# An attention and gated-MLP kernel: more products of ones ahead of the steps, the last tile in three pieces, and a new order of all steps

## The chip, the cores and the metric

The kernel runs on one core of a Trainium2 chip. The metric is device time of one execution in microseconds (us). A core has a matrix engine (TensorE, PE in the profile, with its weight loads shown apart as PEld), a vector engine (VectorE, DVE), a scalar engine that evaluates functions (ScalarE, ACT), a general engine (GpSimd, POOL) and a queue that here issues all transfers (SyncE, SP). Each works through its own queue in order, and they wait for each other by semaphores.

## The reference

Eight batches, each with eight heads of 576 positions and 64 channels. Attention is linear: the softmax of q runs over a row's 64 channels, that of k over the 576 positions, and the 64 by 64 matrix of k and v is formed before q meets it. The result of all heads, 576 by 512, goes through a gated MLP whose gate mixes positions.

```python
q_s = softmax(q, over channels); k_s = softmax(k, over positions)
kv  = einsum('bhsd,bhse->bhde', k_s, v)
x   = einsum('bhsd,bhde->bhse', q_s, kv)       # laid out as (8, 576, 512)
h   = gelu_tanh(x @ w_in)                      # 512 -> 1024
u, v = h[..., :512], h[..., 512:]
v_n = (v - mean(v)) / sqrt(var(v) + 1e-6) * g_ln
v_s = einsum('ts,bsd->btd', w_sg, v_n) + b_sg[None, :, None]
out = x + (u * v_s) @ w_out
```

## The kernel before, in words

Everything is written as small steps, one Python function each, and a table of text, PLAN, names the steps in the order in which they are issued, with their numbers (batch, head or tile) and sometimes a letter for the engine (V is DVE, A is ACT, G is POOL). Each engine's queue is in the order of that table: DVE, ACT, POOL and SP are chained by the class InOrder (line 154 of the profile's rows), and TensorE by `mm` (line 241). So the table decides what stands behind what, and waits between engines follow from which step reads or writes which tile.

The dense products run in a reduced form of float32 with each operand split into a high and a low part, so a product is three products (`x_h` by `wi_h`, `x_h` by `wi_l`, `x_l` by `wi_h`). For each batch the steps are: `load_q`, `load_k`, `load_v`; the softmax steps `q_max`, `q_sub`, `q_exp`, `q_sum`, `q_inv`, `q_mul`, `q_turn` and `k_sub`, `k_exp`; `kv_mm` with `kv_inv` and `kv_scale`; `x_mm` with `x_high` and `x_low`; `hv_mm` and `hv_gelu` for the half v, its normalisation, `hu_mm` and `hu_gelu` for the half u; `sg_mm` and `gate` for the mixing of positions; `out_mm`, `out_add`, `out_rest` and `out_store`. The steps of several batches are interleaved.

Batches 0 and 1 start differently, since nothing else can cover them. For batch 0, `k0_max`, `k0_less` and `k0_mm` take the maximum of k over positions, the exponential (on ACT) and a transposition on TensorE by products with the identity `eye`; `k0_copy` brings the result from PSUM to SBUF. `q0_turn` transposes q in the same way and `q0_copy` copies it. `x0_mm`, `x0_high`, `x0_neg`, `x0_low` form x and its two parts. The weights `w_in` come in eight pieces, which `wi_a` (ACT), `wi_b`, `wi_d` (DVE), `wi_h` and `wi_l` turn into a high and a low part; `wi_x` does one of them on TensorE. The u half of batch 0 is made by `hu0_mm f j s`: tile f of four, half j of the positions, half s of the channels. Four calls with one f fill one PSUM tile, and `hu0_gelu f j` (ACT) reads half j of that tile. All early exponentials on ACT (`k0_less`, `q_exp`) stand ahead of the first gelu, which needs another function table (ACT_TABLE_LOAD).

PSUM is held in three tiles of two banks (`ps2`, shown as ps_0_78, ps_1_79 and ps_2_80) and two of one bank (`ps1`, ps_0_81 and ps_1_82), taken in turn by `bank`. A wait stands between a reader of such a tile and its next writer, also where they touch different halves of it.

Ahead of all steps TensorE multiplies a tile of ones (`vn_1[0]`, set by POOL) with itself 18 times; nothing reads the result. At the end, tile 3 of the last batch's output is made in two halves of 288 columns by `last_mm`, `last_add` and `last_store`, both in one PSUM tile.

Of the kernel before, what the change touches and what calls it, by code (L numbers as in the profile page):

```python
# [38 lines left out]
load_w_in 2, k0_copy 0 2, k0_less 0 1, q0_mul 1 1, wi_a 3, wi_b 3, load_v 0 0, neg, q0_turn 1 1, q0_copy 1 1, load_w_in 0, kv_mm 0 1, k0_copy 0 0
q0_turn 0 0, kv_inv 0 1, q0_copy 0 0, kv_scale 0 1, q0_mul 1 0, wi_a 2, wi_d 1, load_q 1 0, wi_d 3, k0_mm 0 1, k0_copy 0 1, q0_turn 1 0, load_q 1 1  # L40
x0_mm 1 1, load_w_in 6, x0_high 1 1, kv_mm 0 0, wi_b 2, wi_d 2, kv_inv 0 0, x0_neg 1 1, q0_copy 1 0, load_w_in 7, x0_mm 1 0, kv_scale 0 0
x0_low 1 1 A, wi_h 3 V, x0_high 1 0, wi_h 1 V, wi_l 1, x0_mm 0 1, x0_mm 0 0, wi_h 2 V, x0_neg 1 0, wi_x 2, x0_high 0 1, x0_neg 0 1, load_w_in 5
x0_low 1 0 A, hu0_mm 1 0 1, hu0_mm 1 1 1, q_max 1 0, q_max 1 1, wi_a 0, wi_b 0, q_swapm 1 0, x0_low 0 1 A, hu0_mm 1 1 0, load_w_in 4, q_top 1 0
load_k0 1 1, wi_d 0, wi_h 0 V, x0_high 0 0, x0_neg 0 0, wi_x 0, wi_l 3, wi_a 6, q_sub 1 0 V, wi_l 2 A, hu0_mm 3 0 1, hu0_mm 3 1 1, x0_low 0 0 A
wi_l 0 A, q_swapm 1 1 G, wi_b 6, wi_a 4, q_top 1 1, q_exp 1 0, wi_d 6, wi_h 6, hu0_mm 1 0 0, q_sub 1 1 V, q_exp 1 1, load_k0 1 0, wi_b 4, hu0_mm 2 0 1
hu0_mm 2 0 0, hu0_mm 2 1 1, wi_d 4, load_k0 1 2, load_k0 1 3, k0_max 1 2, wi_h 4, k0_less 1 2, k0_max 1 3, k0_less 1 3, load_v 1 1, k0_max 1 1
k0_less 1 1, k0_max 1 0, hu0_mm 3 1 0, wi_l 6, hu0_mm 2 1 0, hu0_mm 3 0 0, wi_l 4 V, q_sum 1 0, q_swapd 1 0 G, k0_less 1 0, hu0_gelu 2 0, hu0_gelu 1 0
q_sum 1 1, q_swapd 1 1 G, q_inv 1 0, load_w_out 2, hu0_gelu 3 0, hu0_gelu 2 1, hu0_gelu 1 1, load_w_sg 2, hv_mm 0 2, hv_mm 0 3, load_w_out 0
k0_mm 1 0, q_mul 1 0 1 V, q_turn 1 1, hu0_gelu 3 1, k0_mm 1 1, hv_gelu 0 2 A, hv_gelu 0 3, k0_mm 1 3, q_inv 1 1, hv_mm 0 0, q_mul 1 1 0, load_g
k0_copy 1 1, load_w_out 1, k0_copy 1 0, wo_a 0, load_kt 2 1, q_mul 1 0 0 V, q_turn 1 0, hv_gelu 0 0 A, q_turn 1 2, load_v 1 0, k0_mm 1 2, load_w_out 3  # L50
k0_copy 1 2, wo_b 0, k0_copy 1 3, wo_d 0, wo_a 2, q_mul 1 1 1, kv_mm 1 0, kv_inv 1 0, kv_scale 1 0, kv_mm 1 1, q_turn 1 3, x_mm 1 0, load_q 2 0
hv_sq 0 0, wo_b 2, hu0_mm 0 0 1, load_v 2 0, kv_inv 1 1, kv_scale 1 1, x_high 1 1, wo_d 2, hv_sq 0 2, x_high 1 0, x_low 1 1, hu0_mm 0 1 1, load_w_sg 3
hv_stat 0 2 A, x_low 1 0, hv_mm 0 1, x_mm 1 1, hv_gelu 0 1, load_q 2 1, x_high 1 2, hv_stat 0 0 A, hu0_mm 0 1 0, load_w_sg 1, hv_stat 0 3, hv_norm 0 3
load_w_sg 0, hv_stat 0 1, hv_norm 0 2, load_kt 2 0, hv_pow 0 2, x_low 1 2, x_high 1 3, x_low 1 3, ws_h 0, hv_norm 0 0, hv_pow 0 3, ws_l 0 V
hv_high 0 2, load_b, hv_low 0 2, hv_high 0 3, hv_low 0 3, load_w_sg 4, hu0_mm 0 0 0, hu0_gelu 0 0, ws_h 2, load_k 2 0, hv_mm 0 4, hv_gelu 0 4 A
hv_norm 0 1, hv_pow 0 0, hv_high 0 0, hv_mm 1 1, hv_gelu 1 1 A, ws_l 2 V, hv_mm 1 2, hv_mm 1 3, hv_low 0 0, b_h, hv_gelu 1 2 A, ws_h 4 V, hv_sq 0 4
hv_pow 0 1, hv_high 0 1, load_k 2 1, kt_max 2 0, ws_l 4, hv_norm 0 4, hv_stat 0 4 A, hv_pow 0 4, tail_high 0, tail_again 0, hv_mm 1 0, kt_max 2 1
tail_low 0, hv_low 0 1, hu0_gelu 0 1, load_kt 2 3, b_l, tail_high 1, load_kt 2 2, q_max 2 1, hv_sq 1 1, q_swapm 2 1, wo_h 0, wo_l 0 V, hv_sq 1 2
hv_stat 1 2 A, hv_norm 1 1, hv_gelu 1 3, sg_mm 0 0, gate 0 0, tail_low 1, kt_max 2 2, sg_mm 0 1, sg_mm 0 2, wo_h 2, hv_gelu 1 0 A, gate_high 0 0
hv_sq 1 0, load_v 2 1, gate 0 2, hv_stat 1 3, gate 0 1, gate_high 0 1, q_top 2 1, sg_mm 0 3, gate_low 0 0, hv_norm 1 2, gate_high 0 2, gate_low 0 1  # L60
hu_mm 1 0, gate_low 0 2 G, kt_max 2 3, hv_pow 1 2, gate 0 3, gate_high 0 3, kt_put 2, hv_stat 1 1 A, hv_high 1 2, hv_stat 1 0 A, hv_pow 1 0
hv_pow 1 3, wo_l 2, hv_norm 1 0, gate_low 0 3, out_mm 0 0, hv_norm 1 3, hu_gelu 1 0, out_mm 0 1, q_max 2 0, q_swapm 2 0, q_top 2 0, out_mm 0 3
out_add 0 0, out_add 0 1, hv_pow 1 1, kt_get 2, hv_high 1 1, k_sub 2 1, out_add 0 3, hv_low 1 2, hv_high 1 0, out_mm 0 2, hu_mm 1 1, load_kt 3 0
hv_low 1 1, hu_mm 1 2, q_sub 2 1 V, q_sub 2 0, out_add 0 2, q_exp 2 0, q_sum 2 0, hv_low 1 0, q_swapd 2 0 G, k_exp 2 1, hu_gelu 1 1, k_sub 2 0
q_exp 2 1, out_rest 0 3, q_inv 2 0, q_mul 2 0 0 V, hv_high 1 3, q_sum 2 1, hu_gelu 1 2, q_mul 2 0 1, q_turn 2 1, k_exp 2 0, hv_low 1 3, q_swapd 2 1 G
kt_max 3 0, load_kt 3 1, kt_max 3 1, load_kt 3 3, kt_max 3 3, q_inv 2 1, out_rest 0 2, out_rest 0 1, load_kt 3 2, kt_max 3 2, tail_again 1, hu_mm 1 3
sg_mm 1 0, kv_mm 2 0, q_turn 2 0, load_k 3 0, q_mul 2 1 0 V, kv_inv 2 0, kv_scale 2 0, q_mul 2 1 1 V, q_turn 2 3, kv_mm 2 1, kt_put 3, hu_gelu 1 3
sg_mm 1 2, gate 1 2, gate 1 0, gate_high 1 2, sg_mm 1 1, gate 1 1, gate_high 1 0, q_turn 2 2, x_mm 2 0, sg_mm 1 3, x_high 2 0, out_rest 0 0
x_high 2 1, kv_inv 2 1, x_low 2 1, x_low 2 0, gate_low 1 0 G, gate_high 1 1, gate_low 1 1 G, gate_low 1 2 G, kv_scale 2 1, gate 1 3, kt_get 3
k_sub 3 0, gate_high 1 3, load_q 3 0, x_mm 2 1, x_high 2 3, gate_low 1 3, load_v 3 0, x_high 2 2, x_low 2 2, out_mm 1 0, x_low 2 3, hv_mm 2 0  # L70
q_max 3 0, q_swapm 3 0 G, load_q 3 1, q_max 3 1, q_top 3 0, out_store 0 0, load_v 3 1, out_store 0 1, q_swapm 3 1, hv_gelu 2 0, q_top 3 1, q_sub 3 0 V
q_exp 3 0, load_k 3 1, out_mm 1 1, q_sub 3 1, hv_mm 2 1, load_kt 4 0, hv_mm 2 3, q_exp 3 1, hv_stat 2 0, kt_max 4 0, q_sum 3 0, k_sub 3 1 G
out_add 1 1, out_store 0 3, q_swapd 3 0, load_kt 4 1, q_sum 3 1, hv_gelu 2 3 A, hv_gelu 2 1 A, q_swapd 3 1 G, hv_sq 2 1, q_inv 3 0, q_mul 3 0 1
q_inv 3 1, out_add 1 0, q_mul 3 1 1, q_mul 3 0 0 V, q_turn 3 0, q_turn 3 3, load_kt 4 2, out_mm 1 3, out_add 1 3, out_rest 1 0, kt_max 4 1, out_mm 1 2
q_mul 3 1 0, k_exp 3 1, kv_mm 3 1, hv_pow 2 0, load_kt 4 3, k_exp 3 0, kv_mm 3 0, out_rest 1 3 V, hv_sq 2 3, hv_stat 2 3 A, q_turn 3 1, hv_norm 2 1
hu_mm 2 3, hv_norm 2 0, hu_gelu 2 3, hv_stat 2 1 A, hu_mm 2 2, kv_inv 3 0, q_turn 3 2, hv_pow 2 1, out_rest 1 1 V, load_k 4 1, out_store 0 2
kv_inv 3 1, kv_scale 3 1, hv_high 2 1, load_k 4 0, hv_norm 2 3, out_add 1 2, kv_scale 3 0, x_mm 3 0, hv_pow 2 3, out_rest 1 2, x_high 3 0, x_low 3 0
x_high 3 1, x_low 3 1, kt_max 4 3, hv_mm 2 2, hu_gelu 2 2, x_mm 3 1, load_q 4 1, hv_gelu 2 2 A, q_max 4 1, x_high 3 3, x_low 3 3, hu_mm 2 1
# [825 lines left out]
```

## Time and profile before

| what | value |
|---|---|
| time, median of 3 runs | 499.36 us (497.37 to 499.56) |
| the profiled execution | 498.94 us, its span 497.2 us |
| TensorE busy | 488.2 us, 98% of the span |
| DVE, ACT, POOL busy | 328.9, 244.3, 167.5 us |
| share of the span on the chain that ended last | PE 93%, DVE 3% |
| bytes moved | 57.28 MB, mean 115 GB/s |

The span runs from the first instruction to the last; 1.7 us of the profiled time lie outside of it. In a row of the timeline the columns are the start in us, the length in us, engine, line, operation, output and inputs by the program's names, and the shape. A row's length covers the first start to the last end of several instructions of one kind, and what stands in brackets is the idle time ahead of it, with the instruction that ended the wait. In a row of windows the columns are the stretch, its length, busy time of each engine with its count of instructions, the granted TensorE clock, the busy share of the transfer engines and GB/s.

### The profile page before, as it was taken

Reading aid. Unit: us, or ns where it says so; the run is one execution under the profiler, and the core shown is the slowest. Engines: PE = TensorE matmul, PEld = TensorE weight load, DVE = VectorE, ACT = ScalarE, POOL = GpSimd, SP = SyncE. Lnnn points to the kernel's source line nnn. Section 1 sums busy time; section 2 is a strip of 40 time slices with the busy share of each in tenths; the row PEclk is TensorE's granted clock in tenths of the full one; section 3 lists DMA queues with packets and bytes.
Section 4 is the critical chain, followed back from the end, with each engine's and each line's share of the span. In section 5 each row is a group of like instructions: output and inputs, shape, how many; then the busy total and the mean of one; then the engine's idle time right before and its main releaser. Section 6 shows DMA issues by size and latency. Waiting matters only on the chain.

```text
span 497.2 us, 9350 instructions
## 1 busy us (share of the span) xinstructions
PE 488.2 (98%) x3852; PEld 448.6 (90%) x3852; DVE 328.9 (66%) x543; ACT 244.3 (49%) x421; POOL 167.5 (34%) x176
## 2 busy tenths in 40 slices
PE   6999999999999999999999999999999999999997
...
GB/s 309 231 398 290 206 171 65 45 26 103 242 135 125 210 130 122 9 170 232 70 49 66 161 176 73 3 102 130 242 1 2 112 9 1 1 24 49 1 25 96
DMA packets 20493, 57.28 MB, mean 115 GB/s; under 512 B 3041, under 2 KB 3425, under 8 KB 20450
## 3 DMA queue, kind: packets, MB, share of 16 engines
...
q14 instruction: 13, 0.11, 0.1%
...
## 4 chain that ended last, share of the span: by engine, by line
PE 93%; DVE 3%; ACT 1%; DMA 1%; issue 1%; POOL 0%; SPq 0%; ACTq 0%; POOLq 0%
PE ps L241 93%; DMA ukt<-kt 1%; DVE k0m L154 1%; DVE o L154 1%; ACT L154 1%; DVE qq L154 0%; DVE qd L154 0%; ACT v L154 0%; ACT kk L154 0%; POOL qq L154 0%; SPq L154 0%; DVE wi_l L154 0%; DVE qm L154 0%; ACT sq L154 0%; ACT nm L154 0%
## 5 line engine op out<-in xcount | busy, mean ns | idle before, releaser
L154 DVE TENSOR_TENSOR u<-ps,u 128x576 f32<-128x576 f32 x32 | 23.8, 754 | 57.0 <-PE ps L241 53.3
L241 PE MATMUL ps<-gh,wo_h 128*128 128x288 f32 x256 | 55.9, 297 | 0.6 <-DVE o L154 0.6
L241 PE MATMUL ps<-gh,wo_l 128*128 128x288 f32 x256 | 55.9, 297 | 0.0
L241 PE MATMUL ps<-ws_h,vnh 128*128 128x288 f32 x256 | 55.3, 297 | 0.0
L241 PE MATMUL ps<-ulow,wo_h 128*128 128x288 f32 x256 | 55.3, 294 | 0.0
L154 ACT CAST gh<-u 128x576 fp32r<-128x576 f32 x32 | 21.1, 672 | 69.5 <-DVE u L154 69.5
L241 PE MATMUL ps<-ws_l,vnh 128*128 128x288 f32 x256 | 54.8, 295 | 0.0
L241 PE MATMUL ps<-ws_h,vnl 128*128 128x288 f32 x256 | 54.8, 295 | 0.0
L154 POOL TENSOR_TENSOR rs<-ve,half 128x1 f32<-128x1 f32 x36 | 25.5, 717 | 77.8 <-DVE ve L154 73.2
L154 ACT ACTIVATE u<-ps 128x576 f32<-128x576 f32 (+2 forms) x36 | 21.1, 602 | 52.4 <-PE ps L241 43.4
L154 POOL TENSOR_TENSOR ulow<-u,gh 128x576 fp32r<-128x576 f32 x12 | 17.6, 1469 | 84.2 <-ACT gh L154 47.4
L241 PEld LDWEIGHTS ps<-ws_h,vnh 128*128 128x128 f32 x256 | 41.8, 188 | 2.3 <-DVE u L154 0.9
L241 PEld LDWEIGHTS ps<-gh,wo_h 128*128 128x128 f32 x256 | 41.6, 188 | 1.8 <-DVE o L154 0.8
L154 ACT ACT_TABLE_LOAD x30 | 38.5, 1283 | 7.8 <-DMA qq<-q 3.7
L241 PE MATMUL ps<-x_h,wi_h 128*128 128x288 f32 (+2 forms) x256 | 42.3, 300 | 0.0
L241 PEld LDWEIGHTS ps<-ws_h,vnl 128*128 128x128 f32 x256 | 41.3, 188 | 0.0
L241 PEld LDWEIGHTS ps<-ulow,wo_h 128*128 128x128 f32 x256 | 41.3, 188 | 0.0
L241 PEld LDWEIGHTS ps<-ws_l,vnh 128*128 128x128 f32 x256 | 41.3, 188 | 0.0
L241 PE MATMUL ps<-x_h,wi_l 128*128 128x288 f32 (+2 forms) x256 | 41.3, 296 | 0.0
L241 PEld LDWEIGHTS ps<-gh,wo_l 128*128 128x128 f32 x256 | 41.3, 188 | 0.0
L241 PE MATMUL ps<-x_l,wi_h 128*128 128x288 f32 (+2 forms) x256 | 41.2, 295 | 0.0
L241 PEld LDWEIGHTS ps<-x_h,wi_h 128*128 128x128 f32 x256 | 36.5, 188 | 3.9 <-ACT u L154 1.8
...
## 6 DMA issues: line engine op xcount, KB each, us to landing
...
```

Of the source, the lines that this page charges most:

```text
L154: ins = op(*args, **kw)
L241: tc.keep_in_program_order(nc.tensor.matmul(*args, **kw))
```

## The change

Three things change.

First, the products of ones. There are 28 ahead of all steps, not 18, and four steps of batch 0 take a new argument that puts such products ahead of their own: one in `k0_mm 0 3 0 1`, three in `kv_mm 0 1 3`, one in `q0_turn 0 0 1`, three in `kv_mm 0 0 3`. They write the PSUM tile that the step then overwrites.

Second, the last tile. Its columns are done in pieces of 288, 144 and 144, each in a PSUM tile of its own.

Third, PLAN is replaced from its first line to its last. The functions of the steps are the same, but their order differs on every engine, and some steps move to another engine: the four early `wi_h` from DVE to ACT, `k0_copy 0 0` and `0 1` from ACT to DVE, one `q0_copy` from DVE to ACT.

```diff
 PLAN = """
-load_q0 0 0, q0_max 0 0, q0_sub 0 0, load_q0 1 1, q0_exp 0 0, q0_max 1 1, q0_sub 1 1, q0_exp 1 1, load_q0 0 1, q0_max 0 1, q0_sub 0 1, load_k0 0 3
...
+load_q0 1 0, q0_max 1 0, load_q0 0 1, q0_max 0 1, load_k0 0 2, k0_max 0 2, load_q0 0 0, load_k0 0 0, q0_sub 1 0, load_k0 0 3, q0_max 0 0, load_q0 1 1
...
+load_v 1 1, k0_less 1 0, hu0_mm 1 1 0, q_sum 1 1, hu0_mm 2 1 1, hu0_mm 2 0 0, hu0_mm 1 0 0, q_swapd 1 1 G, hu0_gelu 3 1, load_w_out 0, load_kt 2 0
+hu0_mm 3 0 0, hu0_gelu 3 0, hu0_mm 2 1 0, load_v 1 0, hu0_gelu 1 0, load_g, load_w_out 2, hu0_gelu 1 1, hv_mm 0 2, hv_gelu 0 2 A, hv_mm 0 3
...
 """
...
-    G.memset(f32(vn_1[0]), 1.0)
-    for i in range(18):
-        mm(ps1[0], vn_1[0][:, 0:P], vn_1[0], start=True, stop=True)
+    ones = vn_1[0]
+    G.memset(f32(ones), 1.0)
+
+    def busy(ps, n):
+        for i in range(n):
+            mm(ps, ones[:, 0:P], ones, start=True, stop=True)
+
+    busy(ps1[0], 28)
...
-    def k0_mm(b, p, both=0):
+    def k0_mm(b, p, both=0, n=0):
         ps, t = flat(bank(ps2, "k0", b, p)), kt0(b, p)
+        busy(ps[:, 0:DV], n)
...
-    def kv_mm(b, h):
+    def kv_mm(b, h, n=0):
 
         kk, vv, pk = kk_s(b, h), vv_s(b, h), sums(bank(ps1, "kv", b, h))
+        busy(st["kv", b, h], n)
...
+    def last_columns(j):
+        return slice(*((0, HS), (HS, HS + HS // 2), (HS + HS // 2, S))[j])
+
     def last_mm(b, j):
-        if not j:
-            bank(ps2, "o", b, 3)
-        pairs = out_pairs(b, 3)
+        es, cs = slice(3 * P, 4 * P), last_columns(j)
+        ps = bank(ps2, "last", b, j)[:, 0, 0:cs.stop - cs.start]
+        hi, lo = wo_hl()
+        pairs = []
+        for d in range(4):
+            gh, gl = gated(b, d)[:, cs], u_s("low", b, d)[:, cs]
+            pairs += [(hi[:, d, es], gh), (hi[:, d, es], gl), (lo[:, d, es], gh)]
         for m, (l, r) in enumerate(pairs):
-            mm(st["o", b, 3][:, j, 0:HS], l, r[j], start=m == 0, stop=m == len(pairs) - 1)
+            mm(ps, l, r, start=m == 0, stop=m == len(pairs) - 1)
```

How the order moves is shown at three places. The first is the head of TensorE's queue. Before (vn is the tile of ones, ukt is k, qq is q, eye the identity):

```order
L241 MATMUL ps_0_81<-vn_71 128x512 x18
L241 MATMUL ps_0_78<-eye,ukt_128 128x128 x5
L241 MATMUL ps_1_79<-eye,ukt_131 128x128 x5
L241 MATMUL ps_2_80<-eye,qq_0_113 128x128 x2
L241 MATMUL ps_2_80<-eye,qq_0_113 128x64
```

And now:

```order
L240 MATMUL ps_0_81<-vn_71 128x512 x28
L240 MATMUL ps_0_78<-eye,ukt_131 128x128 x5
L240 MATMUL ps_1_79<-vn_71 128x512
L240 MATMUL ps_1_79<-eye,ukt_139 128x128 x5
L240 MATMUL ps_2_80<-eye,qq_1_123 128x128 x4
L240 MATMUL ps_0_81<-vn_71 128x512 x3
L240 MATMUL ps_0_81<-vv_1_166,kk_1_168 64x65 x20
```

Ten more products of ones stand first, and four more stand between the early transpositions; the first `kv_mm` (vv by kk) comes after three transposing steps, where it came after five.

The second place is TensorE's queue where the u half of batch 0 ends and its v half begins, with the semaphores that a row waits for. Before, all twelve parts of `hu0_mm` (x_h, x_l by wi_h, wi_l) stand ahead of `hv_mm` (wi by x, 512 wide); these are the last ones:

```order
L241 MATMUL ps_2_80<-x_h_270,wi_h 128x320 x2
L241 MATMUL ps_2_80<-x_h_270,wi_l 128x320 x2
L241 MATMUL ps_2_80<-x_l_307,wi_h 128x320 x2
L241 MATMUL ps_1_79<-x_h_270,wi_h 128x256 x2
L241 MATMUL ps_1_79<-x_h_270,wi_l 128x256 x2
L241 MATMUL ps_1_79<-x_l_307,wi_h 128x256 x2
L241 MATMUL ps_0_81<-wi_h,x_h_270 128x512 [waits Activation_49]
```

And now:

```order
L240 MATMUL ps_1_79<-x_l_332,wi_h 128x256 x2
L240 MATMUL ps_0_78<-x_h_281,wi_h 128x256 [waits Activation_49]
L240 MATMUL ps_0_78<-x_h_281,wi_h 128x256
L240 MATMUL ps_0_78<-x_h_281,wi_l 128x256 x2
L240 MATMUL ps_0_78<-x_l_332,wi_h 128x256 x2
L240 MATMUL ps_2_80<-x_h_281,wi_h 128x320 x2
L240 MATMUL ps_2_80<-x_h_281,wi_l 128x320 x2
L240 MATMUL ps_2_80<-x_l_332,wi_h 128x320 x2
L240 MATMUL ps_0_81<-wi_h,x_h_281 128x512 x4
```

The last but one part, `hu0_mm 3 0 0`, now stands behind `hu0_gelu 3 1` in PLAN. Both use the PSUM tile ps_0_78, so TensorE's row waits for a count of ACT's semaphore, and this count is the one that `hu0_gelu 3 1` reaches. One more part and both `hv_mm` stand behind it in the queue.

The third place is ACT's queue ahead of that gelu. Before:

```order
L154 CAST wi_h<-o 128x2x4x128 [waits DVE_49]
L154 ACTIVATE kk_1_430<-kk_1_430,k0m 128x576 [waits DMAHW7_49,DVE_49,Activation_49]
L154 ACTIVATE kk_1_430<-kk_1_430,k0m 128x576 [waits DMAHW0_49,DVE_49]
L154 ACTIVATE kk_0_363<-kk_0_363,k0m 128x576 [waits DMAHW5_49,DVE_49,Activation_49]
L154 ACTIVATE kk_0_363<-kk_0_363,k0m 128x576 [waits DMAHW6_49,DVE_49]
L154 ACT_TABLE_LOAD
L154 ACTIVATE u_2_471<-ps_2_80 128x256 [waits PE_49]
```

And now:

```order
L153 CAST wi_h<-o 128x2x4x128 [waits DVE_49]
L153 ACTIVATE kk_1_398<-kk_1_398,k0m 128x576 [waits DMAHW5_49,DVE_49]
L153 ACTIVATE qq_0_290<-qq_0_290 128x1152 [waits DMAHW7_49]
L153 ACTIVATE kk_0_411<-kk_0_411,k0m 128x576 [waits DMAHW0_49,DVE_49]
L153 ACTIVATE kk_1_398<-kk_1_398,k0m 128x576 [waits DMAHW6_49]
L153 ACTIVATE kk_0_411<-kk_0_411,k0m 128x576 [waits DMAHW1_49,DVE_49]
L153 ACT_TABLE_LOAD
L153 ACTIVATE u_3_478<-ps_0_78 128x320 [waits PE_49]
```

In both, four `k0_less` and the load of the gelu's table stand ahead of the first gelu. That first gelu is `hu0_gelu 3 1` now, the one that TensorE's row above waits for; before, TensorE's queue had no such row. Over the whole program ACT loads a table 34 times, where it was 30.

More of the change, by code (lines that the diff above doesn't have):

```diff
@@ L39 @@
[L39 to L78, printed above, removed]
@@ L135 @@
-out_store 7 2, out_mm 7 0, out_add 7 0, out_store 7 0, both 7 3 V, last_mm 7 0, last_add 7 0, last_store 7 0, last_mm 7 1, last_add 7 1
-last_store 7 1
+load_q0 1 0, q0_max 1 0, load_q0 0 1, q0_max 0 1, load_k0 0 2, k0_max 0 2, load_q0 0 0, load_k0 0 0, q0_sub 1 0, load_k0 0 3, q0_max 0 0, load_q0 1 1
+q0_exp 1 0, k0_less 0 2, q0_sum 1 0, k0_max 0 0, load_eye, k0_mm 0 2, q0_inv 1 0, k0_max 0 3, q0_sub 0 1, q0_exp 0 1, q0_sub 0 0, q0_mul 1 0
+q0_max 1 1, q0_exp 0 0, load_k0 0 1, k0_less 0 3, load_v 0 1, k0_copy 0 2, k0_less 0 0, q0_sum 0 0, q0_sub 1 1, q0_sum 0 1, q0_exp 1 1, load_w_in 3
@@ new lines @@
+k0_mm 0 3 0 1, load_w_in 2, q0_turn 1 0, q0_inv 0 1, k0_max 0 1, q0_sum 1 1, q0_inv 1 1, k0_copy 0 3, neg, q0_inv 0 0, kv_mm 0 1 3, k0_less 0 1
+k0_mm 0 0, k0_copy 0 0 V, q0_copy 1 0, q0_mul 0 1, q0_turn 0 1, q0_mul 1 1, wi_a 3, kv_inv 0 1, q0_copy 0 1, wi_a 2, k0_mm 0 1, q0_turn 1 1
+kv_scale 0 1, k0_copy 0 1 V, q0_copy 1 1, wi_b 2, load_w_in 1, q0_mul 0 0, wi_a 1, q0_turn 0 0 1, x0_mm 1 0, wi_b 3, q0_copy 0 0, wi_b 1, x0_mm 1 1
+x0_high 1 0, x0_high 1 1, wi_d 3, wi_h 3, load_v 0 0, load_w_in 0, wi_d 1, load_q 1 0, kv_mm 0 0 3, load_q 1 1, wi_d 2, load_w_in 7, wi_a 0, wi_h 2
@@ new lines @@
+kv_inv 0 0, x0_neg 1 0, x0_neg 1 1, wi_h 1, wi_l 1, wi_l 3, wi_b 0, x0_low 1 0 A, wi_x 2, x0_low 1 1 A, kv_scale 0 0, wi_d 0, x0_mm 0 1, x0_mm 0 0
+wi_h 0, x0_high 0 1, q_max 1 0, x0_high 0 0, q_max 1 1, q_swapm 1 1 G, wi_x 0, q_swapm 1 0, x0_neg 0 1, x0_low 0 1 A, q_top 1 0, load_w_in 6
+load_w_in 5, load_w_in 4, q_top 1 1, wi_l 2 A, q_sub 1 1 V, wi_a 6, hu0_mm 3 0 1, hu0_mm 3 1 1, x0_neg 0 0, hu0_mm 3 1 0, load_k0 1 2, x0_low 0 0 A
+q_sub 1 0 V, q_exp 1 1, load_k0 1 3, wi_b 6, wi_d 6, wi_a 4, wi_b 4, wi_d 4, load_w_out 1, k0_max 1 2, load_k0 1 1, hu0_mm 1 0 1, k0_max 1 3, wi_h 6
@@ new lines @@
+wi_l 0 A, wi_h 4, load_k0 1 0, k0_less 1 2, q_exp 1 0, k0_max 1 1, k0_less 1 1, wi_l 4 V, hu0_mm 1 1 1, wi_l 6, k0_less 1 3, hu0_mm 2 0 1, k0_max 1 0
+load_v 1 1, k0_less 1 0, hu0_mm 1 1 0, q_sum 1 1, hu0_mm 2 1 1, hu0_mm 2 0 0, hu0_mm 1 0 0, q_swapd 1 1 G, hu0_gelu 3 1, load_w_out 0, load_kt 2 0
+hu0_mm 3 0 0, hu0_gelu 3 0, hu0_mm 2 1 0, load_v 1 0, hu0_gelu 1 0, load_g, load_w_out 2, hu0_gelu 1 1, hv_mm 0 2, hv_gelu 0 2 A, hv_mm 0 3
+hv_gelu 0 3, q_sum 1 0, q_inv 1 1, hu0_gelu 2 1, q_swapd 1 0 G, q_inv 1 0, q_mul 1 1 1 V, q_mul 1 0 1, hu0_gelu 2 0, load_w_out 3, wo_a 0, load_w_sg 1
@@ new lines @@
+k0_mm 1 0, q_turn 1 3, k0_mm 1 1, k0_copy 1 1, load_w_sg 0, k0_copy 1 0, hv_mm 0 0, hv_gelu 0 0 A, kt_max 2 0, k0_mm 1 3, k0_mm 1 2, q_turn 1 1
+q_mul 1 0 0, q_turn 1 0, k0_copy 1 2, load_q 2 0, wo_b 0, wo_d 0, load_w_sg 2, k0_copy 1 3, kv_mm 1 0, kv_inv 1 0, kv_scale 1 0, kv_mm 1 1, hv_sq 0 0
+q_mul 1 1 0 V, load_w_sg 3, x_mm 1 0, hv_stat 0 0 A, hv_pow 0 0, hv_mm 0 1, wo_a 2, q_turn 1 2, kv_inv 1 1, wo_b 2, wo_d 2, kv_scale 1 1, x_high 1 1
+hu0_mm 0 0 1, load_kt 2 1, x_low 1 1, ws_h 0, ws_l 0, hu0_mm 0 0 0, x_high 1 0, x_low 1 0, hv_sq 0 2, ws_h 2, hv_stat 0 2 A, hv_pow 0 2, x_mm 1 1
@@ new lines @@
+x_high 1 2, x_high 1 3, hv_stat 0 3, load_q 2 1, hv_norm 0 2, hv_norm 0 3, x_low 1 2, x_low 1 3, load_w_sg 4, hv_high 0 2, hv_low 0 2, hv_gelu 0 1
+load_k 2 0, hv_pow 0 3, load_kt 2 2, hv_high 0 3, kt_max 2 1, load_kt 2 3, hu0_mm 0 1 1, hv_low 0 3, hu0_mm 0 1 0, ws_h 4, hv_mm 0 4, hv_stat 0 1
+hv_norm 0 1, hv_gelu 0 4 A, hv_sq 0 4, hu0_gelu 0 0, hv_norm 0 0, hv_stat 0 4 A, hv_pow 0 4, hv_high 0 0, load_v 2 1, hv_norm 0 4, hv_mm 1 1
+hv_gelu 1 1 A, hv_low 0 0, ws_l 4, hv_pow 0 1, q_max 2 0, kt_max 2 3, hv_mm 1 2, kt_max 2 2, hv_gelu 1 2 A, hu0_gelu 0 1, hv_mm 1 0, tail_high 0
@@ new lines @@
+tail_again 0, tail_low 0, load_b, b_h, kt_put 2, hv_mm 1 3, hv_high 0 1, hv_low 0 1, b_l, load_v 2 0, ws_l 2 V, kt_get 2, q_max 2 1, hv_sq 1 1, wo_h 2
+tail_high 1, tail_low 1, sg_mm 0 0, load_k 2 1, hv_gelu 1 3, k_sub 2 1 G, gate 0 0, hv_gelu 1 0 A, hv_sq 1 2, hv_stat 1 2 A, hv_sq 1 0, wo_h 0
+k_sub 2 0, sg_mm 0 2, q_swapm 2 1, sg_mm 0 1, gate_high 0 0, hv_stat 1 3, gate 0 1, hv_norm 1 3, gate 0 2, gate_high 0 2, gate_high 0 1, gate_low 0 0
+hv_stat 1 1 A, gate_low 0 1, load_kt 3 1, wo_l 0 V, hv_norm 1 2, sg_mm 0 3, k_exp 2 0, wo_l 2, q_top 2 1, hv_pow 1 2, k_exp 2 1, gate 0 3
```

147 lines of the change are left out of this document (83 added, 64 removed).

## The prediction

> **What bounds the kernel now.** I read the page first, then busy time by stretches, then TensorE's timeline at both ends, then ACT's.
>
> ```profile
> PE 488.2 (98%) x3852; PEld 448.6 (90%) x3852; DVE 328.9 (66%) x543; ACT 244.3 (49%) x421; POOL 167.5 (34%) x176
> ...
> PE   6999999999999999999999999999999999999997
> ```
>
> ```profile
> 50.00:100.00 50.00, 50.00 (x381) 45.17 (x378) 38.07 (x69) 32.67 (x70) 15.51 (x14) 1.00 0.35 121
> 100.00:200.00 100.00, 99.92 (x822) 91.72 (x822) 72.65 (x120) 59.39 (x93) 43.61 (x47) 1.00 0.43 136
> 300.00:400.00 100.00, 100.00 (x838) 94.08 (x838) 65.34 (x104) 45.10 (x69) 38.16 (x36) 1.00 0.26 84
> ```
>
> From 50 us on TensorE is never without work (0.08 us idle in the second hundred) and its clock is full. There a new order can win nothing; it can only lose, wherever a product finds its data late. What can be won lies in the first 44 us and the last 8. TensorE at the start:
>
> ```profile
> 1.31 6.59 PE L241 MATMUL ps<-vn 128*128 128x512 f32 x18 [1.31 <-POOL vn L154]
> 10.37 1.28 PE L241 MATMUL ps<-eye,ukt 128*128 128x128 f32 x10 [2.47 <-DMA eye<-identity]
> 12.68 1.75 PE L241 MATMUL ps<-eye,qq 128*128 128x128 f32 x6 [1.02 <-POOL qq L154]
> ...
> 17.26 2.43 PE L241 MATMUL ps<-vv,kk 128*64 128x65 f32 x40
> ...
> 27.00 0.40 PE L241 MATMUL ps<-x_h,wi_h 128*128 128x256 f32 x2
> ...
> 29.48 0.40 PE L241 MATMUL ps<-x_h,minus 128*128 128x256 f32 x2
> 29.71 1.03 PE L241 MATMUL ps<-o,eye 128*128 128x512 f32 x2
> ...
> 30.81 0.40 PE L241 MATMUL ps<-x_h,wi_h 128*128 128x256 f32 x2
> ...
> 37.89 1.08 PE L241 MATMUL ps<-wi_h,x_h 128*128 128x512 f32 x4
> 38.81 1.07 PE L241 MATMUL ps<-wi_h,x_l 128*128 128x512 f32 x4
> 40.25 1.17 PE L241 MATMUL ps<-wi_l,x_h 128*128 128x512 f32 x4 [0.37 <-DVE wi_l L154]
> ...
> 44.04 1.80 PE L241 MATMUL ps<-eye,kk 128*128 128x128 f32 x15
> 45.60 1.19 PE L241 MATMUL ps<-wi_h,x_h 128*128 128x512 f32 x4
> ```
>
> The clock falls there (the granted clock is the third column from the right):
>
> ```profile
> 12.00:13.00 1.00, 0.32 (x2) 0.20 (x2) 0.99 (x3) 0.41 (x1) 0.62 (x1) 0.94 1.00 413
> ...
> 16.00:17.00 1.00, 1.00 (x5) 0.51 (x4) 0.90 (x2) 0.00 (x0) 0.61 (x1) 0.50 1.02 412
> ...
> 19.00:20.00 1.00, 1.00 (x17) 0.88 (x14) 0.23 (x2) 0.00 (x0) 0.00 (x0) 0.65 0.07 16
> ```
>
> Half clock from 12.88 (0.94 is 0.12 us at half) to 19.70 (0.65 is 0.70 us at half). The last product of ones had ended at 7.90; until 17.26 TensorE had only transpositions. These kept it busy from 12.68 on, and the clock came back only 2.4 us after the `kv_mm` began. So transpositions alone did not hold the clock, products did.
>
> **The change, part by part.** I follow one marker: the first transposition of batch 1's k (ps<-eye,kk), at 44.04 before. All twelve parts of `hu0_mm` and both `hv_mm` stand ahead of it in both orders.
>
> *Products of ones.* A 512-wide product at full clock takes 0.233 us (0.93 from 37.89 to 38.81, four). Eighteen would take 4.19; they took 6.59, so 2.4 us went to a slow start (the clock column shows 1.00 there, the pace says otherwise). Ten more end at 7.90 + 2.33 = 10.23, just ahead of the 10.37 at which the identity let the first transposition go: hidden by that transfer. If the identity lands earlier, they cost up to 0.6 us of TensorE at a place that waits for ACT later anyway. The eight others (1.9 us) fall into TensorE's early waiting. What they may buy is the half clock: 6.8 us at half, up to 3.4 us.
>
> *The new wait.* `hu0_mm 3 0 0` cannot start before ACT has finished `hu0_gelu 3 1`. So the marker follows ACT. ACT before:
>
> ```profile
> 36.39 1.06 ACT L154 CAST wi_h<-o 128x1024 fp32r<-128x1024 f32 x1
> 37.33 2.80 ACT L154 ACTIVATE kk<-kk,k0m 128x576 f32<-128x576 f32 x4
> 40.15 1.28 ACT L154 ACT_TABLE_LOAD   x1
> 41.44 1.93 ACT L154 ACTIVATE u<-ps 128x256 f32<-128x256 f32 x6
> ```
>
> ```profile
> 16.00:20.30 4.30, 1.29 (x2) 0.57 0.32 127
> ...
> sum 30.15, ACT 24.42; mean ACT 3.49
> ```
>
> ```profile
> L154 ACT COPY kk<-ps 128x640 f32<-128x640 f32 x6 | 4.0, 690 | 0.9 <-PE ps L241 0.9
> L154 ACT ACTIVATE ukt<-ukt,k0m 128x576 f32<-128x576 f32 x4 | 3.0, 767 | 0.8 <-DVE k0m L154 0.8
> L154 ACT CAST wi_l<-ps 128x512 fp32r<-128x512 f32 x2 | 1.2, 596 | 0.0
> L154 ACT ACTIVATE u<-ps 128x320 f32<-128x320 f32 x3 | 1.1, 468 | 0.0
> L154 ACT COPY qt<-ps 128x640 f32<-128x640 f32 x1 | 0.7, 692 | 1.5 <-PE ps L241 1.5
> ```
>
> The sum row is ACT's busy time from 10.00 to 40.15: 24.42 of 30.15 us, so 5.73 idle, 3.01 of it in 16.00 to 20.30, under the half clock. The new order gives ACT, up to the same table load, four `wi_h` of 512 columns (0.55 each, between the 0.60 of its casts and their overlap: +2.2), one `q0_copy` (+0.69), two `k0_copy` less (-1.38), and one more `k0_less` that has not run by 10 us (+0.77; two had before, and now one, since DVE takes the second maximum behind two q steps and a sum). That is 24.42 + 2.28 = 26.7 us of work. With no idle at all the load starts at 36.7 and the gelu ends at 36.7 + 1.28 + 0.47 = 38.45. That is the low end. At the high end ACT keeps as much idle as the half clock gave it, 3.0: 41.5. I take 1.15 of idle, a fifth of what it had, since most waits were for a TensorE at half clock and the rest (data from DVE, transfers) stay: 39.6.
>
> Behind the gelu TensorE still has two parts and both `hv_mm`. Twelve parts took 27.00 to 37.89 less the 1.33 from 29.48 to 30.81: 9.56, so 0.80 each. The `hv_mm` took 44.04 - 37.89 - 0.37 = 5.78. So the marker comes 1.6 + 5.78 = 7.4 after the gelu: 47.0, which is **+2.95** (+1.8 to +4.85). That TensorE gets to its first `hu0_mm` earlier (24 to 27 instead of 27.00) changes nothing in this; ten parts and a small step (8.2 us) later, at 32 to 35, it is dry and waits 3 to 7 us. Break-even is a gelu that ends at 36.65, below the low end.
>
> *The clock after that wait.* Before, 4.8 us with little but transpositions were followed by half clock. Here 3 to 7 us without anything come, so I expect it again. Before, full clock came 2.4 us after the first product at 17.26, and about 5 us after the first of the ones (twice the 2.4 lost). Half of that time is lost: 1.2 to 2.5, I take **+1.85**. If the clock holds, 0. [...]
>
> *The last tile.*
>
> ```profile
> 490.10 0.76 DVE L154 TENSOR_TENSOR o<-ps,o 128x576 f32<-128x576 f32 x1 [2.50 <-PE ps L241]
> ...
> 494.04 0.46 DVE L154 TENSOR_TENSOR o<-ps,o 128x288 f32<-128x288 f32 x1 [1.95 <-PE ps L241]
> ```
>
> ```profile
> 491.29 0.29 PE L241 MATMUL ps<-gh,wo_l 128*128 128x288 f32 x1
> 492.14 0.40 PE L241 MATMUL ps<-gh,wo_h 128*128 128x288 f32 x1 [0.56 <-DVE o L154]
> ...
> 493.71 0.29 PE L241 MATMUL ps<-gh,wo_l 128*128 128x288 f32 x1
> ```
>
> ```profile
> out<-o SPq DMA_DIRECT2D x2, 144.0 KB, 1.8
> ```
>
> The next product could have started at 491.42; it started at 492.14, because both halves shared a tile. That 0.72 goes. In its place 24 products of 144 columns stand for 12 of 288 (0.13 apart). No 144-wide ones are in the trace. Each still needs a weight load of 128 columns; fifteen transpositions of 128 columns took 44.04 to 45.60, 0.104 each, so I take 0.105: 2.5 us, against 0.72 + 1.7. The bounds are 0.066 (half of the wide one) and 0.13. The last addition falls from 0.46 to about 0.31 (0.30 less per 288 columns) and the last transfer is half as large (0.2 less, from 1.8). Net **-0.25** (-1.3 to +0.3). [...]
>
> *The rest of the new order.* Nothing to win, as shown. Each late hand-over costs about the 0.37 or 0.56 seen above. Also ACT loads its table four more times:
>
> ```profile
> L154 ACT ACT_TABLE_LOAD x30 | 38.5, 1283 | 7.8 <-DMA qq<-q 3.7
> ```
>
> That is 5.1 us on an engine that is idle half of the time; uncovered, 1.3 each. I take **+0.3** (0 to 1.5).
>
> **Sum.** 2.95 + 1.85 - 0.25 + 0.3 = +4.85 on the profiled execution of 498.94 us: 503.8. The median of the runs shown is 0.42 above it: 499.36 + 4.85 = **504.2 us**.
>
> **The rivals.**
>
> [...]
>
> 2. The products of ones do not hold the early clock. Four between transpositions are 0.93 us in some 8. Against it: before there was none at all in 9 us. Then ACT keeps its 3 us of idle, the gelu ends at 41.5, and the marker is at +4.85: 499.36 + 4.85 + 1.85 + 0.05 = 506.1.
>
> 3. Faster: ACT reaches the gelu as TensorE runs dry, near 33. Then TensorE does the twelve parts, the small step and the `hv_mm` without a gap from about 24.4: 24.4 + 9.6 + 0.24 + 5.78 = 40.0, four below 44.04, and the time is 499.4 - 4.0 + 0.05 = 495.4. It begins to win below a gelu end of 36.65. Against it: ACT would have to do 26.7 us of work in 21. For it only that early casts might be shorter than their nearest rows.
>
> 4. No change: the gelu at the low end, 38.45, a held clock and a good tail: 1.8 - 0.9 = +0.9, 500.2.
>
> **How the numbers follow.** Forecast 0.52, rivals 0.17, 0.13, 0.08 and 0.10. A measurement of this kernel tells about 0.5% from no change: 496.9 to 501.9. Slower by more: nearly all of the forecast (0.50), 0.11 of rival 1, and rival 2: 0.74. Faster: 0.07 of rival 3. Same: 0.19. All terms at their lowest give 499.8, at their highest 508.5; for 8 in 10 I take 500.3 to 507.2, which leaves out rival 3. The forecast's own range is 502 to 506.5.
>
> **What would show it.** In the changed profile: TensorE idle for 3 to 7 us near 33 to 40, ended by ACT's u (a gelu of 320 columns); that gelu ending at 38.5 to 41.5, right behind a table load; the marker near 47 to 49; a granted clock of 0.5 for some us after the wait and full clock at 13 to 20; the last 24 products about 0.105 apart with no gap. It is wrong if TensorE has no wait of over 2 us there, or if the gelu ends before 36.65.

## The result and the profile after

| | before | changed |
|---|---|---|
| median, us | 498.72 (497.37 to 499.56, 6 runs) | 503.88 (503.44 to 504.38, 6 runs) |
| ratio | | 1.0106 (95%: 1.0089 to 1.0122) |
| profiled execution, us | 498.94 | 504.21 |
| its span, us | 497.2 | 502.4 |

The change makes the kernel 1.1% slower. TensorE does a little more (491.3 us busy, 488.2 before) and waits more. Its timeline in the changed kernel:

```profile
1.31 8.08 PE L240 MATMUL ps<-vn 128*128 128x512 f32 x28 [1.31 <-POOL vn L153]
10.27 0.74 PE L240 MATMUL ps<-eye,ukt 128*128 128x128 f32 x5 [0.89 <-DMA eye<-identity]
...
12.93 1.57 PE L240 MATMUL ps<-vv,kk 128*64 128x65 f32 x40
...
34.38 0.40 PE L240 MATMUL ps<-x_l,wi_h 128*128 128x256 f32 x2
40.47 0.80 PE L240 MATMUL ps<-x_h,wi_h 128*128 128x256 f32 x2 [5.70 <-ACT u L153]
...
43.52 1.91 PE L240 MATMUL ps<-wi_h,x_h 128*128 128x512 f32 x4
45.23 1.15 PE L240 MATMUL ps<-wi_h,x_l 128*128 128x512 f32 x4
...
49.94 1.25 PE L240 MATMUL ps<-eye,kk 128*128 128x128 f32 x10
```

The ten parts of `hu0_mm` that come first are done by 34.8. `hu0_mm 3 0 0` then waits 5.70 us for ACT's u. The last row shown is the marker: 49.94, where it was 44.04. That is +5.90, more than the whole loss. ACT meanwhile (timeline, and its busy time from 10.00 to 38.69 and, of that, from 16.00 to 20.30):

```profile
35.52 1.15 ACT L153 ACTIVATE qq<-qq 128x1152 f32<-128x1152 f32 x1
36.58 2.09 ACT L153 ACTIVATE kk<-kk,k0m 128x576 f32<-128x576 f32 x3
38.69 1.28 ACT L153 ACT_TABLE_LOAD   x1
39.98 0.44 ACT L153 ACTIVATE u<-ps 128x320 f32<-128x320 f32 x1
```

```profile
10.00:38.69 28.69, 26.40 (x44) 1.00 0.94 368
...
16.00:20.30 4.30, 3.65 (x7) 1.00 0.53 188
```

ACT is busy for 26.40 of 28.69 us. The gelu that TensorE waits for ends at 40.42, straight behind the exponentials and the table load. The stretches in which the clock changes, and one from the early stage (the clock is the third column from the right):

```profile
17.00:18.00 1.00, 1.00 (x6) 0.68 (x6) 1.00 (x2) 0.56 (x2) 0.00 (x0) 1.00 0.69 261
...
38.00:39.00 1.00, 0.00 (x0) 0.00 (x0) 1.00 (x1) 0.98 (x3) 0.00 (x0) 0.76 0.85 189
...
45.00:46.00 1.00, 1.00 (x6) 0.77 (x5) 0.57 (x1) 0.00 (x0) 0.00 (x0) 0.82 0.00 0
```

The early half clock is gone. A new one runs from 38.52 to 45.36 (0.76 is 0.48 us at half, 0.82 is 0.36): four `wi_h,x_h` products take 1.71 us to the next row (45.23 - 43.52), where they took 0.92 before. At the end of the program, TensorE:

```profile
495.25 0.29 PE L240 MATMUL ps<-gh,wo_h 128*128 128x288 f32 x1
...
496.85 0.23 PE L240 MATMUL ps<-gh,wo_h 128*128 128x144 f32 x1
496.91 0.27 PE L240 MATMUL ps<-ulow,wo_h 128*128 128x144 f32 x1
...
498.48 0.27 PE L240 MATMUL ps<-gh,wo_h 128*128 128x144 f32 x1
```

There is no gap ahead of the first narrow piece (the twelve wide products take 1.60 us), and the 144-wide products stand 0.112 apart (1.57 us for the 14 from the second to the last one shown). Between the marker and the last tile there is one wait:

```profile
388.67 0.54 PE L240 MATMUL ps<-gh,wo_h 128*128 128x288 f32 x2 [0.46 <-DVE u L153]
```

So the span's +5.2 us splits at the marker: +5.90 ahead of it, -0.7 behind it.

### The profile page after: what moved, and what is told of

The parts are those of the page before. It is cut to its first block, busy times and chain, and to the rows that moved or that the text cites. A ratio compares the mean times of both kernels' runs of the same rounds, so it can differ in the third digit from the quotient of the medians.

```text
span 502.4 us, 9399 instructions
## 1 busy us (share of the span) xinstructions
PE 491.3 (98%) x3882; PEld 452.0 (90%) x3882; DVE 322.3 (64%) x536; ACT 254.2 (51%) x441; POOL 166.1 (33%) x168
## 4 chain that ended last, share of the span: by engine, by line
PE 86%; issue 7%; DVE 2%; POOL 1%; DMA 1%; ACT 1%; SPq 1%; DVEq 0%; POOLq 0%; ACTq 0%
PE ps L240 86%; DMA eye<-identity 1%; POOL kk L153 1%; DVE o L153 1%; SPq L153 1%; ACT kk L153 1%; DVE qm L153 1%; ACT L153 0%; DVE qd L153 0%; POOL qs L153 0%; POOL qe L153 0%; DVE u L153 0%; DVE ulow L153 0%; DVE qq L153 0%; ACT u L153 0%
## 5 line engine op out<-in xcount | busy, mean ns | idle before, releaser
L153 POOL TENSOR_TENSOR rs<-ve,half 128x1 f32<-128x1 f32 x36 | 27.3, 763 | 99.6 <-DVE ve L153 99.5
L240 PE MATMUL ps<-gh,wo_h 128*128 128x288 f32 (+1 forms) x260 | 56.8, 296 | 0.5 <-DVE u L153 0.5
L240 PE MATMUL ps<-ulow,wo_h 128*128 128x288 f32 (+1 forms) x260 | 56.6, 295 | 0.0
L240 PE MATMUL ps<-gh,wo_l 128*128 128x288 f32 (+1 forms) x260 | 56.3, 294 | 0.0
L153 ACT ACTIVATE v<-ps 128x512 f32<-128x512 f32 x36 | 21.3, 598 | 40.9 <-PE ps L240 24.5
```

What stands on the lines that cost most here:

```text
L153: ins = op(*args, **kw)
L240: tc.keep_in_program_order(nc.tensor.matmul(*args, **kw))
```

## The experiments

The theory is the prediction's: the order that puts two parts of `hu0_mm` behind a gelu makes the loss, by a wait and by the half clock that the wait brings. Its rivals are that the new front is slow in itself, that the clock is no term of its own, and that the products of ones matter for the time. A period in the expectations is 3.41 us, half of the 6.82 us at half clock before (12.88 to 19.70). The kernel before was timed again beside each group of runs: 498.95 us in the first group (e1 to e4), 499.05 in the second.

**e1: the two parts ahead of the gelu again.**

```diff
-... hu0_mm 1 0 0, q_swapd 1 1 G, hu0_gelu 3 1, load_w_out 0, load_kt 2 0
-hu0_mm 3 0 0, hu0_gelu 3 0, hu0_mm 2 1 0, load_v 1 0, ...
+... hu0_mm 1 0 0, hu0_mm 3 0 0, hu0_mm 2 1 0, q_swapd 1 1 G, hu0_gelu 3 1, load_w_out 0, load_kt 2 0
+hu0_gelu 3 0, load_v 1 0, ...
```

> The changed kernel with only one thing moved: hu0_mm 3 0 0 and hu0_mm 2 1 0 stand ahead of hu0_gelu 3 1 again, as all parts did before the change. Theory (the wait on ACT's first gelu and the half clock behind it are the loss): the twelfth part ends near 36.0 us instead of 43.5, the wait of 5.7 us is gone, the clock stays full, the marker (first transposition of batch 1's k) comes at 36.0 + 5.8 = 41.8 to 43 instead of 49.94, and the time falls by 7 to 8 us to 496 to 497, 2 to 3 below the kernel before. Rival (the front of the new order is bound by ACT or DVE anyway, and a wait of the same size follows in batch 1's k0_mm, kv_mm or x_mm): TensorE is idle for over 4 us somewhere between 36 and 58 us, and the time stays above 500.

Measured: 496.0 us (495.68 to 496.33), ratio to before 0.9948 (0.993 to 0.9966). TensorE, ACT, one stretch (TensorE's busy time and, behind it, the clock), and all waits of TensorE in the run (in all, times, longest):

```profile
35.55 0.45 PE L240 MATMUL ps<-x_l,wi_h 128*128 128x320 f32 x2
35.84 1.08 PE L240 MATMUL ps<-wi_h,x_h 128*128 128x512 f32 x4
...
41.41 1.25 PE L240 MATMUL ps<-eye,kk 128*128 128x128 f32 x10
```

```profile
38.36 1.28 ACT L153 ACT_TABLE_LOAD   x1
39.65 1.32 ACT L153 ACTIVATE u<-ps 128x320 f32<-128x320 f32 x4
```

```profile
40.00:41.00 1.00, 1.00 (x6) 1.00 1.01 411
```

```profile
PE ps L240 <- POOL vn L153: 1.3, 1, 1.3
PE ps L240 <- DVE u L153: 0.5, 1, 0.5
PE ps L240 <- ACT ukt L153: 0.2, 1, 0.2
```

ACT is as late as in the changed kernel (load at 38.36, there 38.69), but TensorE no longer needs it: `hv_mm` follows the twelfth part at once, and four gelu are done by 40.97, just ahead of the marker, which needs the first bank back. The marker stands at 41.41, the clock holds, and no wait takes the old one's place. The front of the new order is thus faster than the old one by 2.6 us at the marker in these two profiles (41.41 against 44.04); under e7 stands how far that may go with the old order's early half clock. Two entries in one table cost 7.9 us and turned a gain into the loss.

**e2: products of ones inside the wait.** `fill 24` multiplies the ones 24 times into the bank that the next `hv_mm` overwrites.

```diff
-hu0_mm 3 0 0, hu0_gelu 3 0, ...
+fill 24, hu0_mm 3 0 0, hu0_gelu 3 0, ...
```

> The changed kernel with 24 more products of ones (24 x 0.2335 = 5.6 us) on TensorE straight ahead of hu0_mm 3 0 0, into a bank that the next hv_mm overwrites; the wait for the gelu stays, its gap is filled. Theory (the clock is a term of its own): hu0_mm 3 0 0 still starts near 40.5, the granted clock stays 1.00 through 38 to 46, the marker comes 7.4 us after that start, at 47.9 instead of 49.94, and the time falls by about 2.1 us to 501.8. Rival (the slow two steps behind the wait are slow for another reason, such as late operands or ACT): marker stays near 49.9 and the time at 503.9.

Measured: 502.2 us (501.74 to 503.39), ratio 1.0074 (1.0054 to 1.0094).

```profile
34.65 5.65 PE L240 MATMUL ps<-vn 128*128 128x512 f32 x24
40.53 0.51 PE L240 MATMUL ps<-x_h,wi_h 128*128 128x256 f32 x2 [0.23 <-ACT u L153]
...
47.80 1.25 PE L240 MATMUL ps<-eye,kk 128*128 128x128 f32 x10
```

The wait ends at the same time (40.53, 40.47 there), the clock stays at 1.00, and the marker comes 2.14 us earlier. So the half clock is a term of its own: 2.1 us at the marker, 1.7 in the medians. What is left of the +5.90, 47.80 - 44.04 = 3.76, is the wait.

**e3: without the eight products of ones.**

```diff
-k0_mm 0 3 0 1, ... kv_mm 0 1 3, ... q0_turn 0 0 1, ... kv_mm 0 0 3
+k0_mm 0 3, ... kv_mm 0 1, ... q0_turn 0 0, ... kv_mm 0 0
```

> The changed kernel without the eight products of ones ahead of the four early steps; the 28 at the head stay. Theory (the eight hold the early clock, but TensorE has slack there, so the price is only what ACT loses): a granted clock of 0.5 for one or two periods between 13 and 20 us, ACT's gelu 0.5 to 3 us later than 40.42, and the time 504.4 to 507. Rival A (the new order of the front holds the clock by itself, since kv_mm now comes at 12.9): clock full, time 503.9. Rival B (the eight cost more than they bring): gelu earlier, time below 503.4.

Measured: 503.66 us (503.28 to 503.79), ratio 1.0098 (1.0083 to 1.0114). Rival A holds.

```profile
11.91 0.80 PE L240 MATMUL ps<-vv,kk 128*64 128x65 f32 x20
...
39.89 0.79 PE L240 MATMUL ps<-x_h,wi_h 128*128 128x256 f32 x2 [6.24 <-ACT u L153]
...
49.00 1.25 PE L240 MATMUL ps<-eye,kk 128*128 128x128 f32 x10
```

```profile
17.00:18.00 1.00, 1.00 (x7) 1.00 0.31 115
...
37.00:38.00 1.00, 0.00 (x0) 0.58 1.06 308
```

The early clock is full without them (1.00 from 17 to 18 us, behind TensorE's busy time). The whole front comes earlier, the wait for the gelu ends 0.6 us earlier (39.89 against 40.47), and the medians can't be told apart (503.66 against 503.88 us).

**e4: the kernel before, with the wait.** Only the order of three steps of the old table changes.

```diff
-hu0_mm 3 1 0, wi_l 6, hu0_mm 2 1 0, hu0_mm 3 0 0, wi_l 4 V, ... k0_less 1 0, hu0_gelu 2 0, hu0_gelu 1 0
+hu0_mm 3 1 0, wi_l 6, wi_l 4 V, ... k0_less 1 0, hu0_gelu 2 0, hu0_mm 2 1 0, hu0_mm 3 0 0, hu0_gelu 1 0
```

> The kernel before with only two steps moved: hu0_mm 2 1 0 and hu0_mm 3 0 0 stand behind hu0_gelu 2 0, the first gelu, which reads the same bank. Theory (that order alone makes the loss, in either kernel): TensorE runs dry near 36.3, waits until the gelu's end at about 41.9, then 7.4 us of work at a clock that falls to half for about two periods: marker at 41.9 + 7.4 + 2.1 = 51.4 instead of 44.04, time 498.7 + 7.3 = 506. Without the half clock 504. Rival (the loss of the change comes from its new order as a whole): time within 2 us of the kernel before.

Measured: 505.03 us (503.86 to 506.85), ratio 1.013 (1.0102 to 1.0158).

```profile
41.61 0.90 PE L241 MATMUL ps<-x_h,wi_h 128*128 128x320 f32 x2 [5.40 <-ACT u L154]
...
50.56 1.80 PE L241 MATMUL ps<-eye,kk 128*128 128x128 f32 x15
```

```profile
38.00:39.00 1.00, 0.00 (x0) 0.74 1.04 360
...
45.00:46.00 1.00, 1.00 (x5) 0.84 0.16 67
```

The same wait and the same two periods of half clock (38.48 to 45.32) appear in a kernel that has nothing else of the change. The marker is 6.5 us later, the time 6.1 more. From the end of the wait to the marker the work takes 8.95 us (50.56 - 41.61) where 7.4 would do, so the half clock cost some 1.6 us here. With e1 this shows the cause from both sides.

**e5 and e6: e1 with fewer products of ones.** Both leave the eight out; e5 also has 18 at the head.

```diff
-    busy(ps1[0], 28)
+    busy(ps1[0], 18)      # e5 alone
```

> The kernel of e1 (all parts ahead of the gelu) with the products of ones as before the change: 18 at the head, none ahead of the four steps. Theory (the first product behind the ones comes at 11.9 in the new order, and the clock falls only after longer stretches without one; what the ones bring is small): clock full or half for one period only, TensorE at its first hu0_mm within 1 us of e1, time 495.5 to 496.5. Rival (the ten more at the head close the gap to the first transposition and hold the clock; without them it is half for two periods from about 12.9 on): ACT's first gelu 1.5 to 3 us later than the 40.1 of e1, TensorE then waits for it ahead of batch 1's first transposition, time 497 to 499.

> The kernel of e1 without the eight products of ones ahead of the four steps; the 28 at the head stay. From the run without the eight in the changed kernel, where all of the front came about 0.6 to 1.1 us earlier at a full clock: TensorE runs from 1.1 us earlier on, and if batch 1's first transposition finds its bank free (ACT's gelu ends 0.6 earlier too) the marker comes at 40.5 to 40.8 instead of 41.41 and the time is 495.2. Rival (what TensorE gains there, it waits for ACT or DVE later): 496.0.

Measured: e5 496.11 us (495.45 to 496.98), ratio 0.9955 (0.9933 to 0.9978); e6 495.16 us (493.86 to 496.38), ratio 0.9928 (0.9902 to 0.9955). TensorE in e5, and one stretch that ran at half before (the clock is the third column from the right):

```profile
1.31 6.29 PE L240 MATMUL ps<-vn 128*128 128x512 f32 x18 [1.31 <-POOL vn L153]
9.60 0.74 PE L240 MATMUL ps<-eye,ukt 128*128 128x128 f32 x5 [1.99 <-DMA eye<-identity]
...
11.92 0.80 PE L240 MATMUL ps<-vv,kk 128*64 128x65 f32 x20
...
41.85 1.25 PE L240 MATMUL ps<-eye,kk 128*128 128x128 f32 x10
```

```profile
16.00:17.00 1.00, 1.00 (x10) 1.00 0.97 384
```

In e6 the products of ones take longer to begin with, and the marker is still the earliest of all:

```profile
1.31 9.41 PE L240 MATMUL ps<-vn 128*128 128x512 f32 x28 [1.31 <-POOL vn L153]
...
41.05 1.25 PE L240 MATMUL ps<-eye,kk 128*128 128x128 f32 x10
```

With the products of ones as they were before the change, the new order holds the early clock in the profile of e5 all the same and keeps its gain. The three versions e1, e5 and e6 lie within 1 us, and their intervals overlap; e6 has the lowest median of all, 3.9 us below the kernel before.

**e7: the kernel before, with products of ones alone.** 28 at the head, and eight between the early transpositions of the old order.

```diff
-q0_turn 0 1, k0_mm 0 0, ... q0_turn 1 1, ... kv_mm 0 1
+q0_turn 0 1 3, k0_mm 0 0 0 1, ... q0_turn 1 1 3, ... kv_mm 0 1 1
```

> The kernel before with products of ones alone: 28 at the head and eight more between the early transpositions (three in q0_turn 0 1, one in k0_mm 0 0, three in q0_turn 1 1, one in kv_mm 0 1). Theory (the half clock of 6.8 us held back TensorE and ACT): clock full from 6 us on, TensorE at its first steady hu0_mm 1.5 to 3 us before 27.00, time 496 to 497.5. Rival (the front of that order is set by transfers, DVE and ACT, and the half clock lies beside them): first hu0_mm within 0.5 of 27.00, time 498.3 to 499.4.

Measured: 498.02 us (497.69 to 498.52), ratio 0.998 (0.9962 to 0.9997).

```profile
25.71 0.40 PE L241 MATMUL ps<-x_h,wi_h 128*128 128x256 f32 x2
...
29.08 1.13 PE L241 MATMUL ps<-o,eye 128*128 128x512 f32 x2 [0.50 <-DVE o L154]
...
43.50 1.69 PE L241 MATMUL ps<-eye,kk 128*128 128x128 f32 x14
```

What DVE does ahead of that o, in e7 and, in the second fence, before:

```profile
26.62 1.35 DVE L154 TENSOR_REDUCE qm<-qq 128x36 f32<-128x1152 f32 x1 [1.61 <-DMA qq<-q]
```

```profile
27.15 1.35 DVE L154 TENSOR_REDUCE qm<-qq 128x36 f32<-128x1152 f32 x1 [0.85 <-DMA qq<-q]
```

One stretch that ran at half before:

```profile
13.00:14.00 1.00, 1.00 (x7) 0.54 (x5) 0.93 (x6) 1.00 (x3) 0.57 (x1) 1.00 1.01 414
```

The time lies between the theory and the rival. The half clock is gone and TensorE reaches `hu0_mm` 1.3 us earlier (25.71, 27.00 before), but then waits 0.50 for DVE's o, and 0.54 is left at the marker. DVE works in order, and ahead of that o it stands waiting for a transfer of q, which ends the wait only 0.53 us earlier than before (26.62, 27.15). So in this profile the transfer takes back all but half a microsecond.

That is what e7's products of ones brought, not the whole price of the half clock. Of the 34 executions of the kernel before that were timed beside the experiments, 25 have a mean granted clock of 0.990 to 0.993, as its profile with the early half clock has (0.993), and took 498.36 to 500.31 us, median 499.31. The other nine have 0.996 to 1.000, where the profiles without any half clock ahead of the program's end have 0.998 to 1.000 (e1, e2, e5, e6, e7), and took 496.17 to 497.59 us, median 496.85. These nine are 2.5 us below the 25, and 1.2 below e7. Whether the clock itself makes the 2.5 us, or something that comes with it, such as earlier transfers, is not shown: no profile of such an execution was kept. So the early half clock goes with a loss of 0.5 us (e7's profile) to 2.5 us, and against the nine e1 is faster by 0.9 us and not by 3.

**e8: the kernel before, with the last tile alone in three pieces.**

```diff
-last_mm 7 1, last_add 7 1, last_store 7 1
+last_mm 7 1, last_mm 7 2, last_add 7 1, last_add 7 2, last_store 7 1, last_store 7 2
```

> The kernel before with the last tile alone in three pieces of 288, 144 and 144 columns with banks of their own. From its first product to the end of the span the tile took 7.37 us before and 7.15 in the changed kernel. Theory (the pieces bring what they brought there, whatever the order): no gap of 0.72, 144-wide products 0.111 apart, 7.15 +- 0.1, time 0.2 less, 498.5, which the times alone cannot tell from 498.7. Rival (bank or transfer collisions take it back): 7.4 or more.

Measured: 498.92 us (495.81 to 499.35), ratio 0.9992 (0.9967 to 1.0017), which tells nothing by itself. The timeline does:

```profile
489.83 0.30 PE L241 MATMUL ps<-gh,wo_h 128*128 128x288 f32 x1
...
491.42 0.23 PE L241 MATMUL ps<-gh,wo_h 128*128 128x144 f32 x1
```

From 489.83 to the span's end at 497.01 the tile takes 7.17 us. With the ends of the other spans taken to the hundredth (497.16 and 502.43) it took 7.33 before and 7.18 in the changed kernel, so the 7.37 and 7.15 above, from rounded spans, make the gain a little too large. It is 0.16 here, as in the changed kernel (0.15).

## Why the prediction was right

The forecast was 504.2 us, the time 503.88. Term by term, at the marker and behind it:

| term | predicted | measured | from |
|---|---|---|---|
| the new wait | +2.95 (+1.8 to +4.85) | +3.76 | marker of e2, 47.80 - 44.04 |
| half clock behind it | +1.85 (0 to 2.5) | +2.14 | 49.94 - 47.80 |
| last tile | -0.25 (-1.3 to +0.3) | -0.15 | 7.18 against 7.33; e8 |
| rest of the order | +0.3 (0 to +1.5) | -0.5 | 445.31 against 445.79 from marker to last tile |
| sum | +4.85 | +5.25 | span 502.43 - 497.16 = 5.27 |

**The wait** came where it was put, for the reason given, and e1 and e4 show that its place in the order is the cause. Its size was 0.8 too small, inside its bounds. ACT's work was right (26.7 us forecast, 26.40 measured from 10.00 to 38.69); the idle time was not: 1.15 taken, 2.29 measured. That the waiting under the half clock would go was right: from 16.00 to 20.30 us ACT's idle time fell from 3.01 to 0.65. The term that was mis-sized is what stays: a fifth of the 5.73 us was taken, and two fifths stayed. The old trace had 5.73 - 3.01 = 2.72 us of idle time outside of that stretch, so the 1.15 was low by its own rows.

**The half clock** lasted 6.84 us, but its first 1.95 us fell into the wait. The one of e4 (38.48 to 45.32) lasted 6.84 us too, and the one before 6.82 (12.88 to 19.70). How much of the half clock falls behind the wait depends on where it begins (1.95 us ahead of the wait's end here, 3.13 in e4), so the good size of this term (1.6 us in e4, 2.1 here) is in part luck. Rival 1, the wait with a clock that holds (499.36 + 2.95 - 0.25 + 0.3 = 502.4), fell; e2, where the clock was made to hold, gave 502.2.

**The last tile** came out near the forecast: the 144-wide products stand 0.112 apart, where 0.105 was taken from the transpositions.

**The rest of the order** had the wrong sign. One late hand-over of 0.46 us came, of the size and kind that the prediction named, but the stretch from the marker to the last tile was shorter all the same. That is no scatter: from marker to the end of the span the new order takes 452.47 to 452.50 us in the changed kernel, e1, e2, e3, e5 and e6, and the old one 453.12 to 453.14 before, in e4 and in e7. Leaving out the last tile's 0.15 and adding back the hand-over, the new order saves some 0.9 us between the marker and the last tile. Both orders have the same number of products of each shape there. The four further table loads of ACT show no price: behind the marker TensorE waits for nothing but that one hand-over. The claim that a full TensorE leaves a new order nothing to win there is therefore wrong by 0.9 us. The profiles show no single wait that this could be; where it lies stays open. This and the too small wait nearly cancelled, by luck, so a forecast of +4.85 against +5.16 between the medians looks better than its terms.

**The products of ones**: that the ten more are hidden held in the changed kernel (they end at 9.39, the first transposition starts at 10.27); in e6, after a slower start, they end at 10.72, where the identity would have let TensorE go on at 9.60 by e5. That they and the eight hold the early clock was not borne out: e3 keeps it full without the eight, and the profile of e5 without the ten and the eight. Of the up to 3.4 us that removing the half clock might buy, e7 got 0.54 at the marker of the old order; the executions named there put it at 2.5 at most. What holds the clock in the new order is open between two causes that no run separated. `kv_mm` now stands at 12 to 13 us, in the middle of the transpositions, where it was behind them at 17.26; that move stands among the rows ahead of the prediction, which did not draw a conclusion from it. And TensorE is busier: in the 3.41 us ahead of the old order's fall (9.46 to 12.88) it worked for 1.48 us, in the 3.41 us of e5 that end at 12.22 for 2.24.

**The other rivals.** Rival 2 fell, since the early clock was full; rival 4 fell with a gelu that ended at 40.42 and not at 38.45. Rival 3, a faster kernel if ACT reached the gelu near 33, named the right prize by another way: it gave 495.4. ACT did not get faster, but in e1 TensorE no longer asks for it, and the time is 496.0; e6 gives 495.16.
